# A hand-ordered one-core transformer block on Trainium2: another step table, two rows of warm-up matmuls more, and part of the layer-norm moments on GpSimd

## The chip, the cores and the metric

One core of a Trainium2 chip runs the whole program. The metric is device time of one execution in microseconds (us), as the median of several executions. The core has five engines that run side by side, each with an instruction queue of its own that is worked off in order: PE (TensorE, matrix multiplies into PSUM), DVE (VectorE), ACT (ScalarE), POOL (GpSimd, which cannot read PSUM) and SP (SyncE, which here only issues DMAs). An engine waits for another through semaphores.

## The reference, cut to what matters

The input x has 2048 tokens of 448 features; all tensors are bfloat16. Two residual blocks follow one another, each modulated by six vectors worked out from a condition c.

```python
sa, ca, ga, sb, cb, gb = split(silu(c) @ w_mod)      # six vectors of 448
h = layernorm(x) * (1 + ca) + sa
x = x + ga * A(h)        # linear attention
h = layernorm(x) * (1 + cb) + sb
x = x + gb * B(h)        # gated MLP that mixes over the tokens

# A: q, k, v = h @ wqkv, 16 heads of 28
phi(t) = concat(softmax(t @ w_phi), softmax(-(t @ w_phi)))
o = phi(q) @ (phi(k).T @ v) / (phi(q) @ sum(phi(k)) + 1e-6);  A = o @ wo
# B:
z = gelu(h @ w_in);  z1, z2 = z[:, :896], layernorm(z[:, 896:])
B = (z1 * (w_sp @ z2 + b_sp)) @ w_out                # w_sp is 2048 x 2048
```

## The kernel before, in words

The tokens are cut into 16 tiles of 128. The program is a list of 820 words, the string `ORDER` (line 482). Each word names a small function (a step), its tile numbers, the PSUM slot that it fills (`@A0` to `@A2` hold two banks, `@B0` and `@B1` one) and, where there is a choice, the engine: `/V` DVE, `/S` ACT, `/G` POOL, `/Y` SP. The loop at lines 1092 to 1104 runs through the words and issues them. As every engine keeps its own queue, the list fixes two things: the order of the instructions on each engine, and through the slots and buffers which step has to be over before another may write the same place. Nothing else orders the work.

The stages, with the steps that the change and the prediction speak of:

- **The ramp.** Loads `ld:...`; `du` (line 702), matmuls on zeros that compute nothing; `ct` and `ce`, silu of c; for q and k the weights are folded with w_phi: `FT` transposes the raw weights on PE, `ET` copies the result out of PSUM, `bd` lays out w_phi, `PF` multiplies, `EP` copies the folded weight out. `csA`/`ccA` work out sa and 1 + ca as columns, `esA`/`ecA` copy them out (`ecA` is line 743), `SH` applies the shift, `SC` (line 766) scales the four row blocks of Wq, Wk and wv by 1 + ca; block 0 comes out of PSUM, the other three are scaled in place. `l1s`, `l1e`, `l1r`, `l1a` are the first layer norm of a tile; tiles 0 to 3 are turned on PE (`X`, copied out by `XE`), all later ones by a DMA transpose (`T1`).
- **The k stage.** For every tile `kM` and `vM` (4 matmuls each), `kE`/`kF` (exp on ACT), `vC` (copy of v), `kS` and `kR` (sums and reciprocals on DVE), `kP` (line 861, normalises), `kA` (line 868, 8 matmuls that add to kv in PSUM). In between `qM` for q (8 matmuls for each of 8 half blocks of 512 tokens, line 885) with `qE`/`qF` (exp), and `gr`/`ge` for the gates.
- **The passage.** After the last `kA`, `KV` (line 877) masks kv into a block-diagonal matrix; `nM` (line 912, 8 matmuls) gives numerator and denominators of a tile; `nX` (ACT) and `nC`, `nS` (DVE) work out the weights, `nT` (DVE, line 933) multiplies, into two buffers in turn; `nA` adds the two halves, `T2` turns the result by DMA. `SHw` and `SCw` (line 770) shift and scale w_in as `SH` and `SC` do. A slot that `nM` filled is free only when `nT` has read it.
- **The z stage.** `wM`/`wN` (line 945) project by wo; `wN` first adds x by one more matmul with the identity, and then `wR` on ACT only copies out, while after `wM` it is `wR` on DVE that adds x. `wQ` sums squares; `l2R` makes mean and variance of two tiles (`moments`, line 969, 4 small DVE instructions), `l2r` is the power -1/2 on POOL, `l2a` normalises, `T3` turns. `zM` (8 matmuls of 448 columns, line 986), `zG` (gelu with sum, ACT), `zQ` (squares), `zR` and `zW` (moments and power), `zN` (line 1010, normalises) give z2; `yM` (4 matmuls of 512 columns) with `yG` (gelu) gives z1.
- **The g stage.** `W` loads w_sp by DMA transposes; `gM` (16 matmuls) mixes over the tokens for five column chunks by seven feature blocks, `gG` (two DVE instructions) applies b_sp and z1; `oM` (7 matmuls) projects by w_out, `oE` adds x, `oD` stores a tile. `guard` (line 1055) checks the largest softmax sum: four DVE instructions and one matmul.

The two branches of the scaling helper, line 760 on:

```python
if eng is nc.scalar:
    nc.scalar.activation(out=out_, in_=in_, func=ACT.Copy, scale=sc)
else:
    eng.tensor_scalar(out=out_, in0=in_, scalar1=sc, scalar2=None, op0=ALU.mult)
```

## Time and profile before

| | us |
|---|---|
| median of 3 executions | 266.44 (266.23 to 266.92) |
| the profiled execution, its own time | 266.28 |
| its span in the trace | 264.4 |
| mean clock granted to PE | 0.991 |

The span is what the trace covers; 1.88 us of the profiled execution's time lie around it. The profile page gives busy shares of the engines over the whole span. As the stages have different limits, the views that matter are the busy time by stage, the chain of work that ended last (followed back from the last instruction to what released each step), and the timeline of one engine, where the bracket at the end of a row says how long the engine had stood idle and what ended the wait. Matmuls are pipelined: a row of the timeline includes the way out of the array, a row of the chain only the time until the next one, so that the chain's rows are those to add up.

### The profile page before, as it was taken

The numbers are of one execution on the slowest core, as the hardware profiler recorded it, in microseconds if no ns is written. First come the engines' busy times: TensorE is split into PE (matmuls) and PEld (weight loads), VectorE is DVE, ScalarE is ACT, GpSimd is POOL, SyncE is SP. The second block draws the span as 40 slices with busy tenths as digits, with TensorE's granted clock in tenths as the row PEclk, the third lists the DMA queues.
The fourth block names the chain that finished last, engine by engine and source line by source line (L and its number), as shares of the span: only waits on it lengthen the run. The fifth ranks groups of instructions, "written<-read, shape, count | busy, mean of one in ns | idle before, by whom it ended". The sixth has DMA issues, their size and how long they took to land.

```text
span 264.4 us, 4350 instructions
## 1 busy us (share of the span) xinstructions
PE 254.1 (96%) x1632; PEld 138.3 (52%) x1640; DVE 159.1 (60%) x389; ACT 113.2 (43%) x238; POOL 67.6 (26%) x93
## 2 busy tenths in 40 slices
PE   5999999999699999999999999999999999999993
PEld 3864566665445555545444444444444444565771
DVE  4689999966996979877610262435623534335562
ACT  2679987749949998899771000000000100000000
POOL 6227682367632553223362000000000000000000
PEclk9999999999979999999999999999999999999999
DMA  7995999900599561781891000000001397000012
GB/s 183 280 240 117 157 240 250 281 5 13 106 147 174 119 82 41 160 160 42 185 186 29 0 0 0 2 0 0 0 5 35 97 180 132 0 0 30 24 36 80
DMA packets 68656, 25.23 MB, mean 95 GB/s; under 512 B 58129, under 2 KB 68498, under 8 KB 68626
## 3 DMA queue, kind: packets, MB, share of 16 engines
q1 hardware_dynamic: 67088, 22.72, 42.6%
q10 hardware_dynamic: 1538, 2.15, 3.7%
q8 instruction: 15, 0.25, 0.4%
...
## 4 chain that ended last, share of the span: by engine, by line
PE 90%; ACT 3%; DVE 3%; DMA 2%; issue 1%; ACTq 0%; DVEq 0%
PE g_ps L1034 37%; PE z_ps L990 9%; PE z_ps L1018 9%; PE o_ps L1047 8%; PE q_ps L890 5%; PE k_ps L842 4%; PE x_ps L950 4%; PE v_ps L850 4%; PE kvacc L873 3%; PE num L918 2%; DMA f_wq_raw<-in_A_wqkv_dram 2%; DVE f_t L934 1%; PE tps L785 1%; PE sh_ps L758 1%; ACT f_Wq L762 1%; PE pf_ps L801 1%
## 5 line engine op out<-in xcount | busy, mean ns | idle before, releaser
L1034 PEld LDWEIGHTS <-f_z2n 128*128 128x128 bf16 x560 | 50.4, 98 | 47.6
L1040 DVE TENSOR_TENSOR f_gb<-g_ps,f_bsp 128x512 f32<-128x512 f32 (+2 forms) x35 | 20.4, 583 | 58.9 <-PE g_ps L1034 58.7
L1034 PE MATMUL g_ps<-f_Eq,f_z2n 128*128 128x512 bf16 x219 | 48.7, 379 | 0.3
L1021 ACT ACTIVATE f_z1T<-z_ps 128x512 bf16<-128x512 f32 x28 | 16.2, 595 | 71.0 <-PE z_ps L1018 71.0
L1018 PE MATMUL z_ps<-f_hT,f_win 113*128 113x512 bf16 (+1 forms) x112 | 26.4, 379 | 0.0
L990 PE MATMUL z_ps<-f_win,f_hT 112*128 112x448 bf16 (+1 forms) x128 | 26.1, 352 | 0.0
L1034 PE MATMUL g_ps<-f_hT,f_z2n 128*128 128x384 bf16 (+1 forms) x224 | 25.4, 272 | 0.0
L1034 PE MATMUL g_ps<-f_wsp,f_z2n 128*128 128x512 bf16 x109 | 24.5, 379 | 0.2
L1047 PE MATMUL o_ps<-f_wout,f_z1T 128*128 128x448 bf16 x112 | 22.8, 353 | 0.0
L1041 DVE TENSOR_TENSOR f_z1T<-f_gb,f_z1T 128x512 bf16<-128x512 f32 (+2 forms) x35 | 20.5, 585 | 1.9 <-ACT f_z1T L1021 0.5
L990 PEld LDWEIGHTS <-f_hT 112*128 112x128 bf16 (+1 forms) x128 | 12.3, 97 | 11.8
L856 DVE TENSOR_REDUCE f_ksum<-f_E 128x32 f32<-128x896 bf16 x16 | 16.8, 1067 | 0.8 <-ACT f_E L845 0.7
L1050 DVE TENSOR_TENSOR f_xpad<-o_ps,f_x 128x448 bf16<-128x448 f32 x16 | 9.3, 620 | 13.0 <-PE o_ps L1047 12.5
L1018 PEld LDWEIGHTS <-f_win 113*128 113x128 bf16 (+1 forms) x112 | 10.7, 97 | 12.3
L895 ACT ACTIVATE f_Eq<-q_ps 112x1024 bf16<-112x1024 f32 x16 | 16.0, 1034 | 2.7 <-PE q_ps L890 2.7
L934 DVE TENSOR_TENSOR f_t<-num,f_w 128x896 bf16<-128x896 f32 x16 | 16.7, 1084 | 0.2
L994 ACT ACTIVATE f_z2g<-z_ps 128x896 bf16<-128x896 f32 x16 | 14.6, 914 | 3.6 <-PE z_ps L990 3.5
L845 ACT ACTIVATE f_E<-k_ps 128x448 bf16<-128x448 f32 x32 | 15.4, 556 | 1.6 <-PE k_ps L842 0.9
L1047 PEld LDWEIGHTS <-f_z1T 128*128 128x128 bf16 x112 | 10.7, 98 | 9.4
L950 PE MATMUL x_ps<-f_wo,f_oT 112*128 112x448 bf16 x64 | 15.2, 367 | 0.0
L890 PE MATMUL q_ps<-f_hT,f_Wq 113*128 113x512 bf16 (+1 forms) x64 | 14.9, 378 | 0.0
L842 PE MATMUL k_ps<-f_Wk,f_hT 113*128 113x448 bf16 (+1 forms) x64 | 14.1, 352 | 0.0
...
## 6 DMA issues: line engine op xcount, KB each, us to landing
...
```

Source lines behind the costliest of these rows:

```text
L842: nc.tensor.matmul(t[:, 0, 0:D], lhsT=hT[0:KR[m], i, m, :], rhs=Wk[0:KR[m], m, :], start=(m == 0), stop=(m == KC - 1))
L856: nc.vector.tensor_reduce(out=ksum[:, i], in_=Er[i % NR][:].rearrange("p s (c f h) -> p (s c) h f", c=4, h=HP), axis=AX.X, op=ALU.add)
L890: nc.tensor.matmul(t[:, u, :], lhsT=Wq[0:KR[m], m, cc * CB:cc * CB + P], rhs=hT[0:KR[m], 4 * st:4 * st + 4, m, :], start=(m == 0), stop=(m ...
L934: nc.vector.tensor_tensor(out=tr[i % 2][:], in0=numv(i)[:, :, :, 0:DH], in1=wr[i // 2 % 2][:, i % 2].unsqueeze(3).to_broadcast([P, 2, H, D ...
L950: nc.tensor.matmul(t[:, 0, 0:D], lhsT=oT[0:CB, i % 4, cc, :], rhs=wo_s[0:CB, cc, :], start=(cc == 0 and not with_x), stop=(cc == KC - 1))
L990: nc.tensor.matmul(t[:, hf, 0:D], lhsT=hT[0:KR[m], i, m, :], rhs=win_s[0:KR[m], m, FH + hf * D:FH + (hf + 1) * D], start=(m == 0), stop=(m ...
L1018: nc.tensor.matmul(t[:, 0, :], lhsT=win_s[0:KR[m], m, fc * P:(fc + 1) * P], rhs=hT[0:KR[m], 4 * st:4 * st + 4, m, :], start=(m == 0), stop ...
L1021: nc.scalar.activation(out=stage_b()["z1T"][:, fc, st * 512:(st + 1) * 512], in_=ps["y%d_%d" % (st, fc)][:, 0, :], func=ACT.Gelu_apprx_tanh)
L1034: nc.tensor.matmul(g[:, 0, 0:b - a], lhsT=later["z2n"][:, s_, fc * P:(fc + 1) * P], rhs=wspT[t][:, s_, a:b], start=(s_ == 0), stop=(s_ == ...
L1040: nc.vector.tensor_tensor(out=gb, in0=ps["G%d_%d" % (ch, fc)][:, 0, 0:b - a], in1=bsp[:, t * TCHF + a:t * TCHF + b], op=ALU.add)
L1041: nc.vector.tensor_tensor(out=z, in0=gb, in1=z, op=ALU.mult)
L1047: nc.tensor.matmul(ps["o" + str(t)][:, 0, 0:D], lhsT=later["z1T"][:, fc, t * P:(t + 1) * P], rhs=wout_s[:, fc, :], start=(fc == 0), stop=( ...
```

## The change

The string `ORDER` is replaced by another one of 824 words. All steps that compute something are in both; what differs is the order, the slots, the engine letters and the following words.

- The dummies `du` of 1, 8, 7 and 6 matmuls become `du` of 3, 14, 1, 1 and 2, and `dr:4`, a new step of eight matmuls that use half of the rows each.
- `wN` is used for tiles 0, 1, 2, 4 and 8 where it was 0, 1, 2, 3, 6, 7, 10, 11 and 12; the others are `wM`.
- `KV` is split in `KV` and `KZ`, with an engine choice that the table sets to DVE both times.
- `l2R` and `zR` get an engine letter. Of the 16 groups, seven go to POOL (`l2R` of tiles 0, 4 and 8, `zR` of 0, 2, 4 and 8); there the moments take five instructions in place of four.
- Scaling on POOL is written with two operations, add 0.0 and multiply, in place of one. `SCw` on POOL: 1,1 2,1 1,0 2,0 3,1 (before 3,1 and 1,0).
- Other moves between engines: `kP` eight DVE to POOL, two back; `zN` five DVE to POOL, one back; `wR` six ACT to DVE, two back; `wQ` five ACT to DVE, two back; `zQ` three DVE to ACT, two back; `nA` four POOL to DVE, three the other way; `l2a` and `l1a` four each to POOL, two each back; `SCq`, `EP`, `ET`, `XE`, `wos` and `wts` one to three each. Three loads go from the ACT queue to SP's.
- `guard` stands ahead of the first `gM`, where it was late in the g stage.

The ramp, from the first word to where q starts:

```diff
-ld:c/S ld:x0/Y ld:wq/S ld:x1/Y tbl ld:phi/Y m1/V m2a/G du:1@A2 ld:wk/Y ct@B0 ld:x2/Y du:8@A2 m2b/G ce:1 l1s:0 ld:wsa/Y ld:wca/Y ce:2 m3 ce:3 ld:x3/Y
-l1e:0,1/G ce:4 FTq:1@B1 ld:wv/Y m4 l1s:1 ld:x4/Y FTq:0@B0 ETq:1/S du:7@A2 ETq:0/V l1r:0,1 ld:x5/Y bd/V l1e:1,2/V PFq:2@B0 l1a:0/V l1r:1,2 PFq:3@B1
-PFq:1@A2 EPq:2/S ld:wo/Y FTk:0@A1 EPq:3/V EPq:1/S l1a:1/V X:0@B0 W:0,0 FTk:1@B1 l1s:2 XE:0/S X:1@A2 l1s:3 ETk:1/S PFq:0@B0 ETk:0/V l1e:2,4/G EPq:0/S
-csA@A0 XE:1/S l1r:2,4 PFk:2@B0 esA PFk:3@B1 ld:wsb/S SHq@A2 EPk:3/V l1a:3/G ccA@A1 l1a:2/G X:3@B1 ecA PFk:0@A0 EPk:2/V SCq:0/S PFk:1@A1 SCq:1/V XE:3/S
-X:2@B0 EPk:0/V du:6@A2 EPk:1/S l1s:4 SCq:3/S SHk@B1 l1s:5 XE:2/S SCq:2/S SHv@A2 SCk:2/V l1s:6 SCk:1/S qM:0@A1 SCk:0/S SCv:2/V SCk:3/V SCv:1/S SCv:3/V
...
+m3 m2a/V m4 ld:c/S ld:x0/Y l1s:0 m1/V l1e:0,1/V l1r:0,1 l1a:0/G ld:wq/S du:3@A2 ct@B0 tbl ce:1 ld:x1/Y ce:2 ce:3 l1s:1 ld:x2/Y l1s:2 ce:4 ld:phi/Y
+bd/V du:14@A2 FTq:1@B1 ETq:1/S du:1@A2 FTq:0@A2 ETq:0/S l1e:1,2/G l1r:1,2 l1a:1/G l1s:3 l1e:2,4/V du:1@A1 X:0@A1 du:2@A0 dr:4@A0 PFq:1@B0 PFq:2@B1 XE:0/S
+PFq:3@A2 PFq:0@A1 EPq:2/V EPq:1/S EPq:0/S EPq:3/V ld:wk/Y FTk:1@A0 FTk:0@B0 l1r:2,4 l1a:2/V l1a:3/G scb X:1@B1 X:2@A2 ETk:1/S XE:1/S ETk:0/V ld:wsa/Y
+csA@A1 XE:2/V esA PFk:3@B0 PFk:0@B1 PFk:1@A0 PFk:2@A2 EPk:0/S m2b/V EPk:2/V EPk:1/S EPk:3/S ld:wca/Y SHq@A1 ccA@B1 X:3@A2 ecA SCq:3/V SCq:2/V XE:3/V
+SCq:1/S SHk@B0 SCk:3/V SCk:1/V SCq:0/S ld:wv/Y SHv@B1 SCk:0/S SCv:3/V SCv:2/V ld:x3/Y ld:x4/Y ld:wmgb/Y ld:x5/Y l1s:4 l1s:5 l1s:6 l1s:7 l1s:8 l1s:9
+l1s:10 W:0,0 ld:wmga/Y SCv:1/S SCv:0/S l1e:4,8/G l1r:4,8 l1a:4/V l1a:5/G l1a:7/G l1a:6/G T1:4,6 SCk:2/S T1:6,8 qM:0@A2 vM:0@B0 kM:0@B1 kM:1@A1 qF:0
```

The passage:

```diff
-kP:15/V gr:0@B1 kA:15@A0 ge:0 gr:1@B0 KV:0 wos:0/G ccB@B1 ge:1 wos:1/V qM:3@A2 wos:2/G ecB KV:1 wos:3/G csB@B0 qF:3 nM:0@A1 esB nM:1@A0 wts:1/G nX:0
-SHw:3@B0 nC:0 ld:win0/Y nX:1 qE:3 nC:1 SHw:2@B1 nS:0 qM:4@A2 SCw:0,3/V SCw:2,1/S SCw:3,1/G nT:0 SCw:1,1/S nT:1 nA:0/G qM:5@A1 SCw:0,2/S qE:4 nA:1/G
-T2:0,1 qF:4 nM:2@A0 SHw:0@B0 T2:1,2 nX:2 qE:5 nC:2 nM:3@A2 wts:2/G SCw:0,0/V SHw:1@B1 nX:3 qF:5 nC:3 wN:0@B0 nS:1 SCw:1,0/G SCw:0,1/S nM:4@A1 nT:2
...
+KV:1/V KV:0/V ecB KZ:0 KZ:1 esB nM:0@A1 nM:1@A0 qE:3 nX:0 nC:0 nX:1 nC:1 nS:0 nT:0 nT:1 nA:0/V nA:1/V SHw:2@B0 SHw:3@B1 qF:3 SCw:0,2/S SCw:0,3/S
+qM:4@A2 nM:2@A1 nM:3@A0 SHw:0@B0 SHw:1@B1 qF:4 nX:2 nX:3 nC:2 nC:3 nS:1 nT:2 nT:3 nA:2/V nA:3/V SCw:1,1/G SCw:2,1/G wos:1/G wts:4/G T2:0,1 T2:1,2
+W:0,6 T2:2,4 SCw:1,0/G qE:4 SCw:0,0/S SCw:3,0/S SCw:0,1/S qM:5@A2 nM:4@A1 nM:5@A0 wN:0@B0 wN:1@B1 qE:5 nX:4 nX:5 nC:4 nC:5 nS:2 nT:4 nT:5 SCw:2,0/G
+SCw:3,1/G qF:5 nM:6@A2 nM:7@A1 wR:0/S wR:1/S wQ:0/S nX:6 nX:7 nA:4/G nC:6 nA:5/V nC:7 nS:3 nT:6 nT:7 wQ:1/S l2R:0,2/G l2r:0,2 wN:2@B0 wR:2/S wQ:2/S
+qM:6@A0 W:1,2 T2:4,6 l2a:0/V qF:6 qE:6 wM:3@B0 wR:3/V wQ:3/V l2R:2,4/V nA:6/G nA:7/G qM:7@A2 nM:8@A1 nM:9@A0 wN:4@B0 wM:5@B1 zM:0@A2
```

The functions:

```diff
+    def dr(n, slot):
+        wps = bank(slot, "warm_ps")
+        for _ in range(n):
+            for h in range(2):
+                nc.tensor.matmul(wps[:, h, 0:256], lhsT=zero[64 * h:64 * h + 64, 0:P], rhs=zero[64 * h:64 * h + 64, 0:256], start=True, stop=True)
...
     def scale_on(eng, out_, in_, sc):
...
+        elif eng is nc.gpsimd:
+            eng.tensor_scalar(out=out_, in0=in_, scalar1=0.0, scalar2=sc, op0=ALU.add, op1=ALU.mult)
...
-    def moments(a, b, t1, t2, n, nm, v):
+    def moments(a, b, eng, t1, t2, n, nm, v):
+        eng.tensor_scalar(out=nm[:, a:b], in0=t1[:, a:b], scalar1=-1.0 / n, scalar2=None, op0=ALU.mult)
+        eng.tensor_tensor(out=sq[:, a:b], in0=nm[:, a:b], in1=nm[:, a:b], op=ALU.mult)
+        if eng is nc.gpsimd:
+            eng.tensor_scalar(out=v[:, a:b], in0=t2[:, a:b], scalar1=1.0 / n, scalar2=None, op0=ALU.mult)
+            eng.tensor_tensor(out=v[:, a:b], in0=v[:, a:b], in1=sq[:, a:b], op=ALU.subtract)
+        else:
+            eng.scalar_tensor_tensor(out=v[:, a:b], in0=t2[:, a:b], scalar=1.0 / n, in1=sq[:, a:b], op0=ALU.mult, op1=ALU.subtract)
+        eng.tensor_scalar(out=v[:, a:b], in0=v[:, a:b], scalar1=0.0, scalar2=LN_EPS, op0=ALU.max, op1=ALU.add)
```

Besides, one small DVE copy (`maskf`, the mask in float32) is added in the ramp, for the branch of `KV` that the table does not use, and a dummy step `dm` that it does not use either.

More of the change, by code (lines that the diff above doesn't have):

```diff
@@ L554, in fast_path @@
     mask = persist.tile([P, HP], BF, name="f_mask")
+    maskf = persist.tile([P, HP], F32, name="f_maskf")
     KVbd = persist.tile([P, 2, 4, HP, 30], BF, name="f_KVbd")
@@ L919, in nM, with dm @@
                                  rhs=KVbd[0:CB, s, cc, :, :].rearrange("p h d -> p (h d)"), start=True, stop=True)
+    def dm(n, i):
+        for _ in range(n):
+            nc.tensor.matmul(ps["n" + str(i)][:, 1, 480:512], lhsT=zero[:, 0:P], rhs=zero[:, 0:32], start=True, stop=True)
     def nX(i):
```

91 lines of the change are left out of this document (46 added, 45 removed).

## The prediction

> **What bounds the kernel now.** I read the page first, for shares and the chain.
>
> ```profile
> span 264.4 us, 4350 instructions
> ...
> PE 90%; ACT 3%; DVE 3%; DMA 2%; issue 1%; ACTq 0%; DVEq 0%
> ```
>
> The chain is PE for 90% of the span, so the change can win only where PE does not work, or works on nothing. Where that is, the busy time by stage tells (cut at the first q matmul, the end of the k stage, the two ends of a thin place, the end of the z stage and the last matmul; columns: length, PE, PEld, DVE, ACT, POOL, clock).
>
> ```profile
> 0.00:17.90 17.90, 14.34 (x151) 11.19 (x152) 11.52 (x37) 8.76 (x16) 7.61 (x29) 1.00 1.00 251
> 17.90:56.40 38.50, 38.45 (x306) 22.60 (x305) 36.44 (x74) 31.69 (x61) 19.97 (x23) 1.00 0.90 184
> ...
> 65.00:76.40 11.40, 9.23 (x69) 5.40 (x68) 10.25 (x27) 7.93 (x23) 6.79 (x6) 0.85 0.82 116
> 76.40:138.50 62.10, 62.10 (x358) 31.84 (x357) 44.51 (x150) 54.27 (x126) 24.26 (x29) 1.00 0.66 128
> 138.50:260.30 121.80, 121.37 (x681) 62.42 (x687) 50.58 (x90) 3.96 (x7) 1.70 (x2) 1.00 0.16 34
> ```
>
> k, z and g stage are solid PE: 38.45 of 38.50, 62.10 of 62.10, 121.37 of 121.80. No order makes them shorter, it can only tear holes into them. What can be won lies in the 17.9 us of the ramp, in the thin place from 65 on, where the clock falls to 0.85 as well, and in matmuls left out.
>
> **The ramp.** The chain of waits there, then the first useful row of PE:
>
> ```profile
> 5.65 1.74 PE tps L785 x16
> ...
> 8.88 1.13 PE pf_ps L801 x12
> ...
> 11.00 0.58 ACT f_hT L789
> ...
> 14.69 0.17 DVE f_ca L743
> ...
> 14.97 0.63 ACT f_Wq L762
> 15.61 0.48 ACT f_hT L789
> 16.08 0.43 ACT f_Wk L789
> 16.52 0.46 ACT f_Wq L762
> 16.98 0.38 ACT f_hT L789
> ...
> 17.43 0.70 ACT f_Wq L762
> ```
>
> ```profile
> 17.89 1.90 PE L890 MATMUL q_ps<-f_hT,f_Wq 113*128 113x512 bf16 x8
> ```
>
> From 14.97 on ACT alone sets the time: once 1 + ca is there (14.69 + 0.17 = 14.86), it scales three blocks of Wq and copies two turned tiles and one piece of Wk in between, until q starts at 17.89, 3.03 us later. The new table puts behind `ecA` on ACT only SCq:1 and SCq:0 (0.70 + 0.63 = 1.33); SCq:3, SCq:2 and one tile copy go to DVE. DVE takes about 0.33 for a block:
>
> ```profile
> L764 DVE TENSOR_SCALAR f_Wq<-f_Wq,f_ca x1: 327/327/327, 15.3 to 15.3; 112x448 bf16<-112x448 bf16 x1
> ```
>
> A tile copy on DVE is in no trace; the bounds are 0.38 (ACT's shortest step above) and 0.63 (ACT's PSUM block of 448, taken as slow), so DVE has 1.04 to 1.29, beside ACT's 1.33. q then starts some 1.4 after `ecA`: **-1.6**. `ecA` itself comes earlier, I think by 0.6: in the old order the copy of a tile at 11.00 (0.58) stands ahead of that of the turned Wk, on whose heels PF, EP, SH and ccA follow; in the new one it stands ahead of the Wq copies, while ACT waits anyway. Bounds for this half: 0, and -1.4 if the colder half of the start goes faster too. Against it stands the load of x2, now ahead of phi and wk, with DVE's `bd` queued behind the statistics of tile 2: it costs nothing as long as `bd` ends before 8.88, where PF started. Seven `l1s` stand between the scaling on DVE and `l1a:4`, but q, v, k of tiles 0 to 3 (about 9.5 us of PE) cover it. Together **-2.2**, bounds 0 and -3.0.
>
> The dummies are of one piece with this. The 16 transposes at 5.65 took 1.74, 0.109 each, after a break of PE; the 14 new dummies fill that break. The Trainium skill, "TensorE: Matmul & The Clock Gate", Part 1 (the HAM clock gate), says that about 3.4 us of sustained work lift PE to full speed and an idle window of that length drops it. By that rule the transposes would take about half, some 0.8 less; as ET and `bd` stand behind them, I estimate at most 0.4 of it in the end, and the sum below would be 0.4 lower. On the other side the trace shows half speed after a much shorter break, in the thin place, which is next.
>
> **The thin place.** Two rows of PE's timeline with their waits, the streaming times from the chain, and DVE's wait before:
>
> ```profile
> 69.84 0.58 PE L918 MATMUL num<-f_KVbd,f_Eq 112*128 112x120 bf16 x8 [0.22 <-DVE f_t L934]
> 72.37 0.98 PE L918 MATMUL num<-f_KVbd,f_Eq 112*128 112x120 bf16 x8 [1.95 <-DVE f_t L934]
> ```
>
> ```profile
> 67.69 2.09 DVE f_t L934 x2
> ...
> 70.06 0.30 DVE f_opad L940
> ...
> 71.22 1.10 DVE f_t L934
> 72.37 0.98 PE num L918 x8
> 73.35 0.37 PE x_ps L948
> 73.72 1.49 PE x_ps L950 x4
> 75.22 0.37 PE x_ps L948
> ...
> 79.81 0.42 PE num L918 x8
> 80.23 0.76 PE x_ps L950 x4
> ...
> 83.69 0.19 PE x_ps L948
> ```
>
> ```profile
> 65.17 0.19 DVE L925 TENSOR_TENSOR f_cr<-num,f_Sx 128x32 f32<-128x32 f32 x1 [1.88 <-ACT f_Sx L922]
> ```
>
> PE stood 0.22 + 1.95 = 2.17, because `nM` needs a slot that `nT` has not read. After it eight matmuls of `nM` took 0.98 for 0.42, the next five 0.37 + 1.49 for 0.19 + 0.76, one more 0.37 for 0.19: 0.56 + 0.91 + 0.18 = 1.65 lost to the slow clock. In all 3.82. The root is DVE's wait of 1.88 before 65.17: two `qM` were queued on PE ahead of `nM:2`, so DVE had no numerator to work on and was late from then on. The new table queues one `qM` and two `SHw` between pairs of `nM`, and takes both SCw blocks off DVE. A pair costs DVE 71.22 - 67.69 = 3.53 with one `nA`, and 3.83 with the second one (0.30) that comes to DVE. PE has per pair two `nM` (0.84), two `SHw` at four matmuls as x_ps (1.52) and one `qM` (1.74, 1.90 less its way out): 4.1, just more. I let 0.4 of waits stand and no slow clock: **-3.4**, bounds -3.8 and 0.
>
> In this passage POOL gets five SCw where it had two, in a row, and `nA:4` behind them. What one costs decides a rival:
>
> ```profile
> L764 POOL TENSOR_SCALAR f_win<-f_win,f_cb 112x896 bf16<-112x896 bf16 x2 | 5.1, 2536 | 1.4 <-PE sh_ps L758 1.4
> L1012 POOL TENSOR_SCALAR f_z2n<-f_z2g,f_zm,f_zv 128x896 bf16<-128x896 bf16 x3 | 3.7, 1242 | 0.3
> ```
>
> One operation took 2536 ns on 896 elements, two operations 1242. The new branch writes two, so I take 1.24 (below nothing there is no reason to go; above, 2.54). Then POOL starts at `SHw:3`, some 4.5 after the last `kA`, needs 5 x 1.24 and two gates (half the columns of a `kP`, so some 0.9 by its row below) and is through by 12.5, before `nA:4` is due at about 14.
>
> **What else moves.** Four `wN` become `wM`: four identity matmuls of 0.19 less, **-0.76**; their `wR` go from ACT to DVE. In the k stage six more `kP` go to POOL, net, of about 1.69 each:
>
> ```profile
> L863 POOL TENSOR_TENSOR f_phik<-f_E,f_kr x4: 1686/1687/2056, 24.0 to 48.9; 128x896 bf16<-128x896 bf16 x4
> L863 DVE TENSOR_TENSOR f_phik<-f_E,f_kr x12: 592/617/776, 31.0 to 54.0; 128x896 bf16<-128x896 bf16 x12
> ```
>
> POOL's 19.97 of 38.5 become about 31.5 with two `l1a`; DVE's 36.44 fall by 6 x 0.6 and take gates of `wos`/`wts` back. That is hidden while `kA` asks for each `kP` in turn; for the last four, `kA:12` to `kA:15`, my count leaves under half a us. **0**, bounds 0 and +2.5. In the z stage ACT is the next fullest (54.27 of 62.10) and loses eleven `wR` and `wQ`, takes four back and one `zQ`, net; POOL gets seven moments of five small instructions (the row below; with the gaps some 1.3 in all, against about half of that on DVE), four `zN` and two `l2a`, net: 24.26 becomes about 39. No engine gets fuller than ACT was. But each moment on POOL puts `l2a` or `zN` behind it 0.7 later, and what is later still is T3 and `zM`. I take **+0.8**, bounds 0 and +4.
>
> ```profile
> L812 POOL TENSOR_SCALAR f_rs<-f_mv x4: 234/246/248, 3.8 to 25.7; 128x4 f32<-128x4 f32 x2, 128x1 f32<-128x1 f32 x1, 128x2 f32<-128x2 f32 x1
> ```
>
> Three loads pass from ACT's queue to SP's, where T1 and T2 stand in order; ACT saves their issue, and the transposes have 2 to 3 us until their tiles are due. `guard` needs four DVE instructions after the last `zN`, and PE has nine `yM` (nearly 8 us) queued ahead of it: 0, or up to 2 if that cover were gone. In the tail `oD:14`, `oD:9` and `oD:13` are issued between `oE:14` and `oD:15`, 3 x 0.33 us of SP:
>
> ```profile
> L1053 SPq DMA_DIRECT2D out_dram<-f_xpad x16: 332/332/527, 200.3 to 261.0; - x16
> ```
>
> Seven matmuls of `oM` lie between the two `oE`, so SP is nearly free in time; three transfers ahead of the last may cost something: **+0.2**, bounds 0 and +0.7.
>
> Sum: -2.2 - 3.4 - 0.76 + 0 + 0.8 + 0.2 = -5.36, against the profiled execution's 266.28 (span 264.4 and 1.88 around it): 260.9. The median of the runs is 0.16 above that execution; I state **261.0**.
>
> **The rivals.** *The z stage gives back*: `zM` waits for tiles at most pairs. For it: seven moments on POOL, in order behind `zN`. Against: PE was solid at ACT 87%. At +3.3 in place of +0.8: 263.5. *The change does not do what it says on POOL*: two operations cost as much as one did. Then SCw ends 5 x 1.3 = 6.5 later, `nA:4` holds the buffer that `nT:6` must write, and PE stands about 3.7 at `qM:7`, with the slow clock (1.65) behind it: the passage loses 1.5 in place of winning 3.4, 265.8, no change that can be seen. Against: the row of L1012. *Slower*: POOL and DVE get in each other's way. These rows speak for it:
>
> ```profile
> L976 POOL TENSOR_TENSOR f_v<-f_v,f_mhalf x8: 695/711/1479, 75.6 to 122.2; 128x2 f32<-128x2 f32 x8
> L1012 DVE TENSOR_SCALAR f_z2n<-f_z2g,f_zm,f_zv x13: 506/511/1223, 92.4 to 134.8; 128x896 bf16<-128x896 bf16 x13
> ```
>
> The same instruction takes up to twice as long at times on either engine. With much more on POOL, each of the eight pairs of tiles may reach `zM` one us late: 8 x 1.0 in place of 0.8, 266.28 - 2.2 - 3.4 - 0.76 + 8 + 0.2 = 268.1. It decides from 0.8 us per pair on (6.2 / 8). The Trainium skill, "GPSIMD Engine Reference", section 8 (Key points), states such a rule: GpSimd shares its SBUF interfaces with VectorE and contends with its two-port modes and with instructions of two SBUF inputs. The trace agrees that such stretching occurs, but in one or two rows of each group: the medians stand near the minimum.
>
> **How the numbers follow.** Forecast 0.60; better still (the clock rule, nothing lost in z, about 259) 0.06; z gives back 0.17; POOL unchanged 0.07; slower 0.10. An effect under 0.3%, 0.8 us, cannot be told from none here. Faster 0.60 + 0.06 + 0.17 = 0.83, same 0.07, slower 0.10. The range goes from the sum with its good bounds (-3.0 - 3.8 - 0.76 = -7.6: 258.7) to 264.8, which takes in the z rival with some room and leaves 0.17 out.
>
> **What would show it.** q's first matmul at 15 to 16.5; at the passage no PE wait over 0.5 on `f_t` and a clock of 1.00; L764 on POOL at about 1240 ns; the z stage solid PE, with DVE and ACT no fuller; the last matmul near 255. Wrong would be: waits of PE for hT or f_oT behind POOL's moments, waits of `kvacc` for `f_phik`, or a ramp that waits for x2 at `bd`.

## The result, and the profile after

The changed kernel is slower: 268.4 us (median of 20 runs, 266.39 to 270.01) beside 266.39 us for the kernel before on the same chip; the ratio is 1.0077 with a 95% interval of 1.0056 to 1.0099. Forecast was 261.0, so 7.4 us are to be explained. The profiled execution took 269.68 (span 267.9), 1.3 over its median, so sizes below are settled by runs where they can be. The kernel before, timed anew beside each experiment, took 266.4 to 266.8, so gains between two kernels are given as the difference of their ratios to it times 266.4. Such a gain is uncertain by some 1.0 to 1.2 us, both intervals taken together.

The page of the changed kernel, and its busy time cut into stages (first q matmul, first `qM:3`, first `zM:0`, a mark at 138.5, last matmul; columns: length, PE, PEld, DVE, ACT, POOL, clock, DMA share, GB/s):

```profile
span 267.9 us, 4356 instructions
...
PE 78%; DVE 11%; DMA 3%; issue 3%; POOL 2%; ACT 1%; ACTq 0%; DVEq 0%
```

```profile
0.00:14.70 14.70, 13.01 (x157) 9.46 (x158) 11.26 (x42) 8.80 (x16) 7.81 (x23) 1.00 0.95 240
14.70:55.20 40.50, 38.96 (x305) 22.35 (x305) 38.50 (x71) 31.10 (x60) 31.41 (x31) 1.00 1.07 205
55.20:82.10 26.90, 25.08 (x185) 14.14 (x182) 21.39 (x52) 17.81 (x38) 13.89 (x18) 0.87 0.29 59
82.10:138.50 56.40, 54.84 (x310) 27.66 (x310) 41.60 (x121) 44.56 (x101) 37.24 (x64) 1.00 0.71 123
138.50:261.40 122.90, 122.45 (x686) 62.87 (x692) 48.10 (x85) 6.03 (x11) 0.00 (x0) 1.00 0.18 36
261.40:267.90 6.50, 0.00 (x0) 0.00 (x0) 0.62 (x1) 0.00 (x0) 0.00 (x0) 0.71 0.25 77
```

Three rows of the kernel before, in the same cut, that the prediction did not show:

```profile
17.90:56.25 38.35, 38.30 (x305) 22.51 (x304) 36.29 (x74) 31.54 (x61) 19.82 (x23) 1.00 0.91 184
56.25:82.00 25.75, 23.58 (x186) 13.43 (x183) 19.64 (x54) 19.75 (x41) 16.28 (x15) 0.93 0.56 83
...
260.30:264.40 4.10, 0.00 (x0) 0.00 (x0) 0.62 (x1) 0.00 (x0) 0.00 (x0) 0.85 0.20 66
```

The reader is to see where the time comes and goes. The ramp is 3.2 shorter (17.9 to 14.7). The k stage is 2.15 longer, and PE stands in it for 1.54 (38.96 busy of 40.50; it was 38.30 of 38.35); VectorE is not emptier there by 6 x 0.6 but fuller by 2.2. The passage is 1.15 longer, at a clock of 0.87, which is more than the kernel as a rule pays there, as shown below. From `zM:0` to the last matmul it is 1.0 longer (179.3 beside 178.3), though four matmuls are gone. The tail is 2.4 longer. PE's share of the chain falls from 90% to 78%, and VectorE's rises from 3% to 11%: where nearly nothing but PE set the time, VectorE now sets a tenth of it.

In the k stage GpSimd's work and VectorE's gatings stand side by side (timelines of GpSimd, then of VectorE):

```profile
43.35 3.34 POOL L873 TENSOR_TENSOR f_phik<-f_E,f_kr 128x896 bf16<-128x896 bf16 x2 [0.91 <-DVE f_kr L870]
47.67 3.48 POOL L873 TENSOR_TENSOR f_phik<-f_E,f_kr 128x896 bf16<-128x896 bf16 x2 [0.98 <-PE kvacc L883]
51.83 1.69 POOL L873 TENSOR_TENSOR f_phik<-f_E,f_kr 128x896 bf16<-128x896 bf16 x1 [0.68 <-DVE f_kr L870]
```

```profile
45.38 1.56 DVE L924 TENSOR_TENSOR f_wout<-f_wout,f_g_rep 128x448 bf16<-128x448 bf16 x1
46.86 0.38 DVE L924 TENSOR_TENSOR f_wo<-f_wo,f_g_rep 112x448 bf16<-112x448 bf16 x1
...
47.42 1.02 DVE L866 TENSOR_REDUCE f_ksum<-f_E 128x32 f32<-128x896 bf16 x1
...
48.82 0.79 DVE L924 TENSOR_TENSOR f_wout<-f_wout,f_g_rep 128x448 bf16<-128x448 bf16 x1
49.53 1.07 DVE L866 TENSOR_REDUCE f_ksum<-f_E 128x32 f32<-128x896 bf16 x1
50.53 0.88 DVE L924 TENSOR_TENSOR f_wout<-f_wout,f_g_rep 128x448 bf16<-128x448 bf16 x1
...
52.53 1.24 DVE L924 TENSOR_TENSOR f_wo<-f_wo,f_g_rep 112x448 bf16<-112x448 bf16 x1
```

A gating takes 0.38 when GpSimd is idle (46.86). The other four end at 46.94, 49.61, 51.41 and 53.77. GpSimd's products end, taking each pair as two equal halves, at 46.69, 49.41, 51.15 and 53.52: each gating ends 0.20 to 0.26 behind one. That looks less like two engines sharing a rate than like one waiting for the other's instruction to end. The reductions in between, with one input, take 1.02 to 1.07, no more than elsewhere. Five gatings cost VectorE 4.85 in place of 5 x 0.38 = 1.9, the keys' sums come late, and PE waits:

```profile
53.58 0.59 PE L883 MATMUL kvacc<-f_vaug,f_phik 128*128 128x116 bf16 x8 [1.02 <-POOL f_phik L873]
...
54.82 0.59 PE L883 MATMUL kvacc<-f_vaug,f_phik 128*128 128x116 bf16 x8 [0.27 <-DVE f_phik L873]
55.25 3.01 PE L907 MATMUL q_ps<-f_hT,f_Wq 113*128 113x512 bf16 x8
...
68.63 0.59 PE L935 MATMUL num<-f_KVbd,f_Eq 112*128 112x120 bf16 x8 [1.42 <-DVE f_t L955]
69.62 0.98 PE L935 MATMUL num<-f_KVbd,f_Eq 112*128 112x120 bf16 x8 [0.40 <-DVE f_t L955]
70.40 0.58 PE L969 MATMUL x_ps<-f_x,f_ident 128*128 128x448 bf16 x1
```

Those rows of PE show the passage too: a wait of 1.42, another of 0.40, and matmuls at half speed behind them (0.98 for 0.59). The half speed is not in every execution. Four other kernels have the steps of this passage unchanged (the runs on the tail, the gatings, `zN` and the buffer below): with the same waits of 1.41 and 0.40 they take 24.1 to 24.2 at a clock of 1.00, so 1.6 less than before. A fifth, with fewer dummies, takes 26.0. The row of the run on the tail:

```profile
55.64:79.78 24.14, 22.15 (x185) 12.70 (x182) 21.51 (x53) 17.72 (x38) 14.04 (x18) 1.00 0.37 67
```

VectorE is late in the passage for the same reason as in the k stage:

```profile
61.12 2.00 POOL L772 TENSOR_SCALAR f_win<-f_win,f_cb 112x896 bf16<-112x896 bf16 x2 [7.59 <-PE sh_ps L766]
63.09 1.03 POOL L924 TENSOR_TENSOR f_wo<-f_wo,f_g_rep 112x448 bf16<-112x448 bf16 x1
64.07 1.18 POOL L924 TENSOR_TENSOR f_wout<-f_wout,f_g_rep 128x448 bf16<-128x448 bf16 x1
65.24 3.12 POOL L772 TENSOR_SCALAR f_win<-f_win,f_cb 112x896 bf16<-112x896 bf16 x3
```

```profile
63.23 2.27 DVE L961 TENSOR_TENSOR f_opad<-f_t 128x448 bf16<-128x448 bf16 x2
...
65.73 0.68 DVE L950 TENSOR_TENSOR f_dn<-f_cr 128x32 f32<-128x32 f32 x1
...
66.84 0.60 DVE L952 TENSOR_TENSOR f_w<-f_Sx,f_dn 128x64 f32<-128x64 f32 x1
...
106.52 2.26 DVE L1004 TENSOR_SCALAR f_xpad<-f_x,f_m,f_v 128x448 bf16<-128x448 bf16 x2
```

The two `nA` at 63.23 take 2.27 where two take 0.68 alone, and end at 65.50, 0.25 behind the gating that ends at 65.25. Even the addition of 128x32 at 65.73 (0.19 alone) ends 0.13 behind the first scaling of the last three, at 66.28. The last row is one of the z stage: two `l2a` (0.70 alone) beside two `zN` on GpSimd from 106.48 to 108.65. An `l2a` has one tensor input, but it is a fast operation: 448 columns of bf16 in 0.35, where the reduction above takes 1.02 for 896. The two `nT` at 61.23, which read PSUM, are not held up: 2.09 beside two scalings on GpSimd, and 2.09 in the run below with GpSimd idle.

**Theory.** While GpSimd runs a product, a scaling or a normalisation, VectorE can't run an operation with two SBUF inputs, nor a fast bf16 one; it waits until GpSimd's instruction ends. VectorE comes late, PE waits, and a low clock can follow a long wait. **Rivals.** GpSimd's own slowness is what is late (k stage); the moments on GpSimd make hT late (z stage); the two-operation form is worth nothing; the ramp only moved work behind q. And for the tail: three stores bunched ahead of the last, against a chance of that one execution.

### The profile page after: what moved, and what is told of

It is laid out like the page before. It is cut to its first block, busy times and chain, and to the rows that moved or that the text cites. A ratio compares the mean times of both kernels' runs of the same rounds, so it can differ in the third digit from the quotient of the medians.

```text
span 267.9 us, 4356 instructions
## 1 busy us (share of the span) xinstructions
PE 254.3 (95%) x1634; PEld 136.5 (51%) x1643; DVE 161.5 (60%) x369; ACT 108.3 (40%) x224; POOL 90.4 (34%) x135
## 4 chain that ended last, share of the span: by engine, by line
PE 78%; DVE 11%; DMA 3%; issue 3%; POOL 2%; ACT 1%; ACTq 0%; DVEq 0%
PE g_ps L1059 36%; PE z_ps L1043 8%; PE o_ps L1072 8%; PE z_ps L1015 6%; PE q_ps L907 4%; PE k_ps L852 3%; PE x_ps L971 3%; PE v_ps L860 3%; DVE f_t L955 2%; PE num L935 2%; DVE f_ksum L866 2%; DMA f_wq_raw<-in_A_wqkv_dram 2%; DMA f_hT<-f_xpad 1%; PE kvacc L883 1%; DVE f_opad L961 1%
## 5 line engine op out<-in xcount | busy, mean ns | idle before, releaser
L1046 ACT ACTIVATE f_z1T<-z_ps 128x512 bf16<-128x512 f32 x28 | 15.1, 594 | 46.8 <-PE z_ps L1043 46.8
L873 POOL TENSOR_TENSOR f_phik<-f_E,f_kr 128x896 bf16<-128x896 bf16 x10 | 16.8, 1704 | 2.8 <-DVE f_kr L870 1.8
L855 ACT ACTIVATE f_E<-k_ps 128x448 bf16<-128x448 f32 x32 | 16.1, 556 | 3.2 <-PE k_ps L852 2.3
L907 PE MATMUL q_ps<-f_hT,f_Wq 113*128 113x512 bf16 (+1 forms) x64 | 16.3, 399 | 0.0
```

The lines of the kernel that those rows point to most:

```text
L873: eng.tensor_tensor(out=pr[i % NR][:, 0:2 * D].rearrange("p (a f h) -> p a f h", a=8, h=HP), in0=Er[i % NR][:].rearrange("p s (c f h) -> p ...
L907: nc.tensor.matmul(t[:, u, :], lhsT=Wq[0:KR[m], m, cc * CB:cc * CB + P], rhs=hT[0:KR[m], 4 * st:4 * st + 4, m, :], start=(m == 0), stop=(m ...
```

## The experiments

Each is compared with the kernel before on the same chip. A line "..." stands for tokens left out.

**The ramp on the old table.**

```diff
  m3 m2a/V m4 ld:c/S ld:x0/Y
  ...
  T1:4,6 SCk:2/S T1:6,8 qM:0@A1      (new table up to here)
- vM:0@B0 kM:0@B1 kM:1@A1 qF:0
+ ld:wo/Y ld:wsb/S kM:0@B0 qF:0 vM:0@B1 kE:0        (old table from here)
  ...
```

> The step table of before behind the new ramp: the new order of steps up to q's first matmul, then the rest of the old table with its old engines (moments, key softmax, gates and scalings where before had them). Theory (the ramp gained all that it shows, and the loss sits in the k stage, the passage, the z stage's hT wait and the tail): q's first matmul at 14.9 us again, and the time 2.5 to 3.0 under before, 263.4 to 263.9. Rival (the ramp only moved work behind q's first matmul, and the k stage paid for it): within 0.8 of before, 265.6 to 266.4, with the k stage 2 us longer than in before.

Measured: 271.71 us, ratio 1.0189 (1.014 to 1.0238), k stage 43.2, and q's first matmul at 17.0. Neither number came. PE stood 2.42 and 0.80 for f_hT in the k stage, and the clock was 0.50 over the three microseconds behind the longer of these breaks. The tile that it waited for was issued at 31.79 and took 5.9 to land; the same transpose of the kernel before, issued at 31.09, took 3.0. Why it was so slow is not shown. The run says nothing on the size of the ramp's gain.

**The tail.**

```diff
- oD:10/Y oD:8/Y oD:11/Y oD:5/Y
+ oD:10/Y oD:8/Y oD:11/Y oD:9/Y oD:5/Y
  ...
- oE:14 oE:15 oD:14/Y oD:9/Y oD:13/Y oD:15/Y
+ oE:14 oE:15 oD:13/Y oD:14/Y oD:15/Y
```

> The changed kernel with two output stores moved earlier: tile 9's behind tile 11's, tile 13's ahead of tile 14's, so that only tile 15's is issued after the last addition. Theory (the bunched stores make the tail): last matmul to the end of the span back from 6.5 to about 4.5, the time 1.5 to 2.0 under the changed kernel's. Rival (the tail of the profiled execution was an accident, or the stores wait on the transfers and not on their issue): less than 0.5 gained.

Measured: 266.2 us, ratio 1.0001 (0.9972 to 1.0031), so 2.0 faster than the changed kernel, and the tail 4.2, as the theory had it. SP's rows at the end of the changed kernel and of this one:

```profile
260.74 2.58 SPq L1078 DMA_DIRECT2D out_dram<-f_xpad  x4
```

```profile
258.96 0.33 SPq L1078 DMA_DIRECT2D out_dram<-f_xpad  x1
```

Four issues in a row take 2.58, 0.64 each on the mean where one alone takes 0.33, and from the end of the last issue to the end of the span it is then 4.6 us (267.9 - 263.32), here 3.2 (262.5 - 259.29). It was no chance of one execution, but not the rule without exception either: of the eight profiled kernels with the bunched order six have 4.3 to 4.9 there and two 3.5; the twelve without it have 3.0 to 3.8.

**Three gatings out of the k stage.**

```diff
- wts:3/V wos:3/V
+ wos:3/V
  ...
- wts:0/V kS:14 wts:2/V
+ kS:14
  ...
- wts:1/G
+ wts:1/G wts:2/G wts:0/G wts:3/G
```

> The changed kernel with three of the five gatings on VectorE in the k stage (wts:0, 2, 3) taken to GpSimd in the last stage. Theory (VectorE's two-input bf16 operations are held up by GpSimd's key softmax, and the late VectorE makes PE wait for f_phik): the three cost 3.2 us of VectorE there where 1.15 would do; without them PE's waits of 1.02 and 0.24 go, the k stage falls from 40.5 to 38.5 to 39.3, and the time by 1.2 to 2.0. Rival (GpSimd's own 1.69 us per product, six in a row more than before, sets the k stage): waits on GpSimd's f_phik stay, time within 0.5.

Measured: 267.46 us, ratio 1.0047 (1.0017 to 1.0077), 0.8 faster, which the intervals do not tell from nothing. The stage shows it: 39.3 in this kernel and in the three later ones without these gatings, 40.5 to 41.4 in the eight that have them. PE's waits for GpSimd's f_phik are down from 1.3 in two (1.02 the longest) to 0.3, with GpSimd's products unchanged at 1.69. So most of it was VectorE's lateness and not GpSimd's length; the gain is less than I expected, and 0.9 of the stage's excess stays.

**GpSimd idle in the passage.**

```diff
- SCw:1,1/G SCw:2,1/G wos:1/G wts:4/G
- SCw:1,0/G
- SCw:2,0/G SCw:3,1/G
```

> The changed kernel without seven of GpSimd's steps in the passage: the scalings SCw:1,1, 2,1, 3,1, 1,0 and 2,0 and the gatings wos:1 and wts:4 are left out (that part of the weights stays unscaled), so that GpSimd is idle from 55 to 73 us while PE's and VectorE's instructions stay the same. Theory (VectorE's two-input bf16 and f32 operations wait while GpSimd works): the two nA at 63 take 0.7 together where they took 2.27, the two additions of nS 0.2 where they took 0.68 and 0.60, PE's waits of 1.42 and 0.40 for f_t go, and with them the stretch of low clock at 70 to 74; the passage is 1.5 to 2.5 shorter. Rival (VectorE's order alone makes nT late, or the clock falls anyway at 69): the waits stay and the passage is within 0.5 of the changed kernel's.

Measured: 265.73 us, ratio 0.997 (0.9933 to 1.0006), 2.85 faster. The kernel leaves these scalings and gatings out. The passage takes 22.85: 4.0 less than in the changed kernel's profile, 1.3 less than where that passage ran at full clock (24.1), and 2.9 less than before. VectorE's rows:

```profile
62.41 0.68 DVE L960 TENSOR_TENSOR f_opad<-f_t 128x448 bf16<-128x448 bf16 x2
...
63.79 0.19 DVE L949 TENSOR_TENSOR f_dn<-f_cr 128x32 f32<-128x32 f32 x1
```

0.68 for 2.27 and 0.19 for 0.68; PE's waits for f_t fall to 0.2, and the clock is 1.00. So VectorE's order alone does not make `nT` late, and that rival is out. Of the 4.0, some 2.7 came with the clock, which fell in the profile and not in each execution.

**GpSimd's instructions cut in two.**

```diff
-            eng.tensor_scalar(out=out_, in0=in_, scalar1=0.0, scalar2=sc, ...)
+            for v in (slice(0, FH // 2), slice(FH // 2, FH)):
+                eng.tensor_scalar(out=out_[:, v], in0=in_[:, v], scalar1=0.0, scalar2=sc, ...)
```

and `kP` on GpSimd likewise, in two pieces of 448 columns.

> The changed kernel with each of GpSimd's key softmax products and scalings in the passage cut into two instructions of half the columns, the same work in the same order. Theory (VectorE's operation with two inputs from SBUF waits until the GpSimd instruction that is running ends: in the changed kernel such operations ended 0.12 to 0.28 after one): the waits shrink with the instruction, so no gating in the k stage takes over 1.3 us (1.56 and 1.24 before), the two nA at 63 us together at most 1.8 (2.27), and the time falls by 0.3 to 1.2, GpSimd's own overhead of some 0.1 per extra instruction taken off. Rival (the two engines share a bandwidth, so that VectorE runs slower while GpSimd works, however its work is cut): the same stretched durations, time the same or up to 0.8 longer.

Measured: 267.49 us, ratio 1.0028 (0.9999 to 1.0057), 1.3 faster, though the k stage itself took 41.4: a product in two pieces takes GpSimd 1.9 in place of 1.7. GpSimd's row and VectorE's gatings in the k stage:

```profile
45.08 3.77 POOL L877 TENSOR_TENSOR f_phik<-f_E,f_kr 128x448 bf16<-128x448 bf16 x4 [0.89 <-DVE f_kr L871]
```

```profile
47.12 0.92 DVE L927 TENSOR_TENSOR f_wout<-f_wout,f_g_rep 128x448 bf16<-128x448 bf16 x1
47.97 1.12 DVE L927 TENSOR_TENSOR f_wo<-f_wo,f_g_rep 112x448 bf16<-112x448 bf16 x1
```

The four pieces end at 46.02, 46.97, 47.91 and 48.85; the gatings end at 48.04 and 49.09, 0.13 and 0.24 behind the last two. No gating takes over 1.12 now (1.56 and 1.24 in the changed kernel). This speaks for waiting and against a shared rate, which would not care how the work is cut. The two `nA` still took 2.14, not 1.8 at most: they stand beside GpSimd's two gatings, which I had left whole.

**All mended, first try.** The stores and `wts:0`, `2` and `3` as above, GpSimd's scalings in halves as above (its products whole), and:

```diff
- wos:1/G wts:4/G      (wts:4 to the last stage)
+ KZ:1 wos:1/V
- nA:0/V nA:1/V nA:2/V nA:3/V
+ nA:0/G nA:1/G nA:2/G nA:3/G
- kA:15@A0 qM:3@A2 csB@B0
+ csB@B0 kA:15@A0 qM:3@A2
```

> The changed kernel with all that the theory blames mended, and the whole computation done: output stores as in the earlier run (2.2 gained there), the gatings wts:0, 2, 3 and 4 in the last stage (0.9 gained there for three), wos:1 on VectorE while it waits for PE, nA:0 to 3 on GpSimd, its scalings in halves, and csB's matmuls ahead of the last kvacc. Theory: 268.4 less 2.2, less 1.0 to 1.3 in the k stage, less 1.0 to 2.5 in the passage (2.7 with GpSimd idle there), 262.4 to 264.2, under before. Rival (the gains overlap, since a late PE hides a late VectorE elsewhere): 264.8 to 266.4, no better than before.

Measured: 266.26 us, ratio 0.9986 (0.9957 to 1.0015). The rival's number. PE's list of waits says why:

```profile
PE q_ps L908 <- DVE f_t L956: 1.5, 1, 1.5
PE z_ps L1016 <- DMA f_hT<-f_xpad: 1.3, 1, 1.3
```

`nA:4` stood on GpSimd behind ten half scalings, so `nT:6` could not write its buffer; and the wait of the z stage was not touched.

**All mended, second try.** The stores, `csB`, `wos:1` and `nA:0` to `nA:3` as in the first try, the scalings whole again, and:

```diff
- SHw:2@B0 SHw:3@B1 qF:3
+ qE:3 SHw:3@B1 SHw:2@B0 nX:0
- SCw:1,1/G SCw:2,1/G SCw:1,0/G SCw:2,0/G SCw:3,1/G
+ nT:1 SCw:1,1/V nA:0/G nA:1/G
+ nT:3 SCw:1,0/V nA:2/G nA:3/G SCw:2,1/G SCw:3,1/G
+ nA:4/G SCw:2,0/G
- zN:4/G zN:5/G
+ zN:4/V zN:5/V
  ...
- wts:3/V wts:0/V wts:2/V wts:4/G
+ zN:9/V wts:3/V wts:0/V wts:2/V wts:4/V
```

> The changed kernel with the whole computation done and what the theory blames mended a second time: stores spread and csB ahead of the last kvacc as in the run before; wos:1, SCw:1,1 and SCw:1,0 on VectorE where it waits for PE or ScalarE, wts:0, 2, 3 and 4 on VectorE after the attention; nA:0 to 3 on GpSimd with SCw:2,1 and 3,1 behind them and 2,0 behind nA:4; and zN:4 and 5, beside which two l2a took 2.25 us on VectorE in place of 0.70, on VectorE. Theory: the wait for f_t behind GpSimd's nA:4 (1.5) and the wait for hT near 110 us (1.3) of the mended kernel go, time 262.5 to 264.3. Rival (each wait taken away uncovers the next, and VectorE's own work is the bound): 265.0 to 266.5.

Measured: 262.82 us, ratio 0.9832 (0.9764 to 0.9899): 6.5 faster than the changed kernel and faster than the kernel before. Behind the ramp no wait of PE is over 0.7, and its clock stays at 1.00 through the passage of 23.1:

```profile
55.20:78.30 23.10, 21.76 (x167) 12.34 (x165) 19.86 (x52) 17.58 (x38) 14.24 (x19) 1.00 0.44 71
```

**Fewer dummies.**

```diff
- du:14@A2 FTq:1@B1
+ du:6@A2 FTq:1@B1
  ...
- du:2@A0 dr:4@A0
```

> The changed kernel with fewer dummies in the ramp: du:14 cut to du:6, du:2 and dr:4 left out, nothing else moved. Theory (the dummies bring the clock up before the first transposes, and that is what the ramp gained): PE's clock is below 1 until the weights' products, q's first matmul at 15.5 to 17.5 us in place of 14.7 to 15.9, time 0.5 to 2.0 longer. Rival (the order of the loads and the two engines that share the ramp's copies gained it): q's first matmul within 0.4 and the time within 0.6 of the changed kernel's.

Measured: 270.61 us, ratio 1.0128 (1.0093 to 1.0163), 1.4 slower than the changed kernel; q's first matmul at 17.4 in the profile, which took 272.99. Transposes of the changed kernel, then of this one:

```profile
5.43 0.62 PE L795 MATMUL tps<-f_ident,f_wq_raw 112*112 112x112 bf16 x8 [0.19 <-DMA f_wq_raw<-in_A_wqkv_dram]
...
9.02 0.99 PE L795 MATMUL tps<-f_ident,f_wk_raw 112*112 112x112 bf16 x16
```

```profile
6.45 1.00 PE L795 MATMUL tps<-f_ident,f_wq_raw 112*112 112x112 bf16 x8 [2.52 <-DMA f_wq_raw<-in_A_wqkv_dram]
...
11.16 1.70 PE L795 MATMUL tps<-f_ident,f_wk_raw 112*112 112x112 bf16 x16
```

Eight transposes take 1.00 in place of 0.62 behind a break of 2.52, sixteen later ones 1.70 in place of 0.99, and PE is slow until 12.65. The granted clock in these stages reads 1.00 all the while, so durations have to be read here, not that column. The dummies are worth 1.4 in time. How much of the ramp that is, the profile does not settle, since wq landed 1.0 later in it: with all of the dummies and a late wq (5.9 and 6.3), two other kernels of this ramp also started slowly and had q's first matmul at 17.2 and 17.0.

**Dummies alone in the kernel before.**

```diff
- du:8@A2
+ du:14@A2
```

> The kernel before with one part of the change: du:8 made du:14, so that PE works until wq has landed. Theory (PE's clock is low after the break of 1.23 us, and that is most of what the ramp gained): the 16 first transposes 1.2 in place of 1.74, q's first matmul at 15.2 to 16.4 in place of 17.9, and the time 1.0 to 2.5 less. Rival (what the ramp gains is waited for again in the k stage, as when the new ramp stood ahead of the old table): q's first matmul early, time within 0.6 of before.

Measured: 266.45 us, ratio 0.9972 (0.9941 to 1.0003): at most a small gain. The 16 transposes took 1.58 and q began at 17.29: ahead of the dummies PE still stood 0.80 for the row of c, and the transposes at 5.85 were slow without any break before them. The changed table has three dummies ahead of that place, too; whether they are what is missing here was not tested.

**And the two-operation form.**

```diff
+        elif eng is nc.gpsimd:
+            eng.tensor_scalar(out=out_, in0=in_, scalar1=0.0, scalar2=sc, op0=ALU.add, op1=ALU.mult)
```

> The run with du:14 in the kernel before, and the two-operation form of GpSimd's scaling as well: its two scalings of 2.53 us in the passage become about 1.0 (three of them took 3.12 in the changed kernel). Theory (VectorE waits until the GpSimd instruction ends, and nA:0 and nA:1 stand behind them on GpSimd): the passage 0.3 to 1.5 shorter than with du:14 alone. Rival (nobody waits for these scalings): within 0.3 of it.

Measured: 266.05 us, ratio 0.9969 (0.9935 to 1.0003), the same as without it. In the changed kernel the form took 1.01 at the median of five where one operation took 2.54, so it does what it says; in the old table it gains nothing that these runs can tell.

**Moments back on VectorE.**

```diff
- l2R:0,2/G l2R:4,6/G l2R:8,10/G zR:0,2/G zR:2,4/G zR:4,6/G zR:8,10/G
+ l2R:0,2/V l2R:4,6/V l2R:8,10/V zR:0,2/V zR:2,4/V zR:4,6/V zR:8,10/V
```

The kernel moves all seven, one more (`zR:2,4`) than the expectation lists.

> The changed kernel with the moments that went to GpSimd back on VectorE: l2R of 0,2, 4,6 and 8,10 and zR of 0,2, 4,6 and 8,10. Theory (the moments on GpSimd are worth nothing either way on the mean, their chain only delays hT once by 1.2 to 1.3): the wait of PE for hT near 112 us goes, VectorE has 3.9 us more to do where PE is the bound, time 0 to 1.2 less. Rival (VectorE is full in the z stage, so that they were worth moving): PE waits for hT or z2n there, time 0.5 to 2.0 longer.

Measured: 277.21 us, ratio 1.0418 (1.0342 to 1.0495), 9.1 slower. The rival, and far beyond its number: the new table fills VectorE in the attention (18.2 of the 20 us from 80 to 100 in the changed kernel), and 5.3 us more of work on VectorE (166.8 busy in place of 161.5) make PE wait 3.0 each for f_t and f_oT, once for 2.30 with half the clock behind it. In this table the moments were worth moving.

**Moments alone, and their control.** In the table of before, six moments, then five on GpSimd, then none of them but the changed source around that table.

```diff
- l2R:0,2/V l2R:4,6/V l2R:8,10/V zR:0,2/V zR:4,6/V zR:8,10/V
+ l2R:0,2/G l2R:4,6/G l2R:8,10/G zR:0,2/G zR:4,6/G zR:8,10/G
```

> The table of before with one part of the change: the moments l2R and zR of 0,2, 4,6 and 8,10 on GpSimd, in five operations each, in their old places. Theory (the moments are small operations of 0.2 us, so they block VectorE little, and PE is the bound in the z stage): within 0.6 of before. Rival of the prediction (their longer chain on GpSimd makes hT or z2n late): 0.8 to 3 longer, with PE waiting for f_hT.

> The table of before with five of the six moments on GpSimd: l2R:0,2, the one that falls into the passage, stays on VectorE. Theory (the moments in the z stage cost nothing, as the stage was 178.23 beside 178.28 with all six; what the six cost came from the passage): within 0.5 of before. Rival (each moment on GpSimd costs): 0.6 to 1.5 longer, and the z stage with it.

> The control for the two runs with moments alone: the table of before, all moments on VectorE, in the changed source (a cast of the mask on VectorE of 0.25 us in the ramp, KZ as a step of its own). Theory (the moments cost nothing in the z stage and the 1.1 to 1.4 of those runs came with the source): 0.8 to 1.6 over before. Rival (the moments themselves cost it): within 0.5 of before.

Measured: 268.24, 267.93 and 268.96 us, ratios 1.0041 (1.0004 to 1.0078), 1.0053 (1.0028 to 1.0079) and 1.0084 (1.0054 to 1.0114). The first two alone read as a cost of the moments, though the z stage had kept its length (178.2 and 178.3 from `zM:0` to the last matmul, 178.3 before). The control turns it round: the changed source costs the table of before 2.2 us without any moment moved. With the moments on GpSimd it is 0.8 to 1.1 less, which the intervals do not tell from nothing; a cost of theirs is not to be seen.

**The z stage's wait.**

```diff
- zN:4/G zN:5/G
+ zN:4/V zN:5/V
```

> The changed kernel with zN:4 and zN:5 on VectorE, as before had them, nothing else. Theory (the wait of PE for hT near 112 us comes from the two l2a that VectorE can't start beside GpSimd's two zN): the pair of l2a takes 0.7 in place of 2.26, the wait of 1.2 to 1.4 for f_hT falls under 0.4, and the time by 0.5 to 1.5. Rival (the chain of moments and rpow on GpSimd makes hT late): the wait stays over 0.8, time within 0.4.

Measured: 267.42 us, ratio 1.0014 (0.9979 to 1.0049), 1.7 faster. The same two `l2a`:

```profile
105.36 0.70 DVE L1004 TENSOR_SCALAR f_xpad<-f_x,f_m,f_v 128x448 bf16<-128x448 bf16 x2
```

0.70 for 2.26, and PE's wait for f_hT 0.5 for 1.3, with the moments still on GpSimd. So their chain is not the cause of the wait. The stretched `l2a` is one cause, and accounts for 0.8 of the 1.7; the other is how late the turned tile lands, which comes next: without the buffer the two `l2a` still took 2.33, and PE waited 0.2.

**What the source costs.** Beside the moved steps, the changed source has a buffer `f_maskf` (128x4 in f32, 16 bytes a partition) and a cast into it, which no step of the table reads.

```diff
-    maskf = persist.tile([P, HP], F32, name="f_maskf")
...
-        nc.vector.tensor_copy(out=maskf[:], in_=mask[:])
```

Out of the changed kernel, out of the mended one, and, of the control, the cast alone:

> The changed kernel without its f_maskf: the cast of the mask on VectorE in the ramp and its buffer of 16 bytes a partition, which nothing reads. Theory (the control lost 2.2 by this source alone, so the changed kernel does too): 1.0 to 2.5 faster than the changed kernel. Rival (the control lost it in the order of before only, where a late tile of hT meets q in the k stage): within 0.6 of the changed kernel.

> The kernel with everything mended a second time (262.8), without f_maskf as well. Theory: another 0.5 to 2.0 faster, 260.8 to 262.3. Rival: within 0.5 of 262.8.

> The control once more, the table of before in the changed source, without the cast and with the buffer f_maskf, which shifts the buffers allocated after it by its 16 bytes a partition. If the instruction costs the 2.2, the time is that of before within 0.5; if the place of the buffers does, it stays 1.5 to 2.5 over before.

Measured: 267.39, 262.18 and 268.52 us, ratios 1.0012 (0.9971 to 1.0053), 0.9825 (0.9767 to 0.9884) and 1.0065 (1.0034 to 1.0096). The changed kernel gains 1.7 without buffer and cast; the mended one 0.2 by the ratios (0.6 by the medians), which is the rival's number and not told from nothing; and the control without the cast stays 1.7 over before. So the cast is not needed for the cost, and the buffer is what is left, beside the split of `KV`, which the control has too. What speaks for the buffer is that the turned tiles land later, and that PE waits for one in the control's passage, as it never does in the kernel before:

```profile
PE x_ps L968 <- DMA f_oT<-f_opad: 1.2, 1, 1.2
```
From issue to landing, median, of the kernel before, of the control with the buffer only, of the changed kernel, and of the changed kernel without it:

```profile
f_hT<-f_xpad SPq DMA_TRANSPOSE x15, 2.8
...
f_oT<-f_opad SPq DMA_TRANSPOSE x9, 2.8
```

```profile
f_hT<-f_xpad SPq DMA_TRANSPOSE x15, 3.5
...
f_oT<-f_opad SPq DMA_TRANSPOSE x9, 3.5
```

```profile
f_hT<-f_xpad SPq DMA_TRANSPOSE x15, 3.4
...
f_oT<-f_opad SPq DMA_TRANSPOSE x9, 3.1
```

```profile
f_hT<-f_xpad SPq DMA_TRANSPOSE x15, 2.8
...
f_oT<-f_opad SPq DMA_TRANSPOSE x9, 2.7
```

The same holds for all kernels of this study: the five without the buffer have 2.7 to 2.8 in both rows, the fifteen with it 3.3 to 3.9 for f_hT and 3.0 to 3.5 for f_oT. The Trainium skill, "DMA: Bandwidth & Descriptors", section "DMA Transpose (X-bar)", gives 32-byte alignment in SBUF for a transposed move; 16 bytes ahead of the other buffers could break it. The runs agree in direction; the addresses were not read, so that the alignment is the cause is argued and not shown.

The kernel mended and without the buffer, at 262.18 us, is the fastest of all, 1.75% under the kernel before, though not told apart from the one with the buffer.

## Why the prediction was wrong, step by step

Against the sum, the k stage came 2.15 too long, the passage 1.8 where it ran at full clock and 4.5 in the profile, the z stage with the matmuls 1.0, the tail 2.2; the ramp came as forecast or better.

**The ramp, -2.2.** It came: -3.2 in the profile, -1.8 to -2.7 in nine other kernels of this ramp (q's first matmul at 15.2 to 16.1), less in the two named above. How it splits is known only in part. I gave 1.6 to work taken off ScalarE and at most 0.4 in the end to the dummies, and the dummies alone are worth 1.4 in time. The row was there: 16 transposes took 1.74 where the changed kernel needs 0.99. I let the half speed end with them; in the run with few dummies it went on for 6 us, through the weights' products.

**The passage, -3.4.** The balance was right: 4.1 us of PE a pair against 3.8 of VectorE, no slow clock, is what the run with GpSimd idle shows (22.85, -2.9). With GpSimd at work it was -1.6 at full clock and up to +1.1 with a low one. The step that failed is "what one costs decides a rival": I priced the scalings on GpSimd alone (1.24 each, they took 1.01) and checked only whether GpSimd was through before `nA:4`, which it was. That VectorE stands still meanwhile, PE waits 1.4 and 0.4 for it and the clock can fall behind that, was not in the sum: 2.85 of time, by that run.

**The k stage, 0 (bounds 0 and +2.5).** +2.15, inside the bounds. "DVE's 36.44 fall by 6 x 0.6" failed: it rose to 38.50, because five gatings beside six more products took 4.85 in place of 1.9. Without three of them the stage was 1.2 shorter.

**The z stage, +0.8 (0 to +4), and the four matmuls, -0.76.** Together +1.0 in place of 0. The size is not far off, which was luck, as the mechanism is another: not the moments' chain but two `zN` that held up two `l2a` (1.7 by the run that moved them, 0.8 of it seen in the stage) and a turned tile that landed late. The moments that I priced at +0.8 pay in the new table: back on VectorE they cost 9.1.

**The tail, +0.2 (0 to +0.7).** +2.4 in the profile, 2.0 by the run. The mis-sized term is "three transfers ahead of the last may cost something": an issue in a row costs 0.64 on the mean, not 0.33, and the last store lands later.

**Not in the sum: the buffer.** The diff shows `f_maskf`, and I costed every instruction but no address: 1.7, cast and buffer together, inside the stages above.

**The rivals.** "POOL and DVE get in each other's way" had a chance of 0.10 and 268.1 us, and that is the kind of what happened, at nearly that time; but it was placed in the z stage at 1 us for each of eight pairs. It acts in the k stage, the passage and once in the z stage, where a long GpSimd instruction stands beside the wrong kind on VectorE. I set it low as "the medians stand near the minimum" in the kernel before. That was no evidence: there, the two engines seldom worked side by side on such operations, and the stretched row was one that did (L1012 on VectorE took 1223 ns at 92.38, beside an `nA` on GpSimd from 92.25 to 93.35, and 511 at the median). The range stopped short of it.

The Trainium skill, "SBUF — State Buffer", section "Who interferes with whom", says it outright, and the prediction does not weigh that page: VectorE and GpSimd share a pair of ports as an exclusive lock, held for a whole instruction; two-input operations and the two-port modes of copies and scalings need it, reductions do not. The rows agree on these points: ends 0.12 to 0.26 behind GpSimd's, shorter waits when its instructions are cut, `ksum` untouched. The lock works the other way too: GpSimd's `l1a` at 31.62 took 1.17 in place of 0.71 beside a `kP` of VectorE that took its usual 0.62. Two details go further. Beside GpSimd's power (`l2r` and `zW`, 0.7 each) VectorE was not held up in the changed kernel: two `l2a` at 112.02 took 0.70, an `nA` at 104.51 took 0.38. And in the first mended kernel an addition waited past one end and ran behind the second of GpSimd's queued pieces, taking 1.03.
